# Masking one bank of scores on VectorE, computing it last, and moving the input sums in an attention and feed-forward kernel

## The chip, the cores and the metric

The kernel runs on one core of a Trainium2 chip. The metric is the device time of one execution in microseconds (us). Three runs of the kernel before took 1059.14, 1061.83 and 1064.9 us, so the median is 1061.83 us. TensorE (PE in the profile, with PEld for its weight loads) does the matrix products, ScalarE (ACT) the exponentials and copies out of PSUM, VectorE (DVE) reductions and subtractions, GpSimd (POOL) masks and other elementwise work, and SyncE (SP) issues nearly all transfers (DMAs).

## What is computed

One block with two parallel branches on a normalized input. Everything in it is float32; the attention is causal with a window of 256 keys.

```python
S, D, H, W, Df = 2048, 640, 32, 256, 1728
xn = layernorm(x)
q, k, v = split_heads(xn @ wqkv)                      # 32 heads of 20
scores = einsum("bhqd,bhkd->bhqk", q, k) * 20 ** -0.5
mask = (i - j >= 0) & (i - j < 256)
o = softmax(where(mask, scores, -1e9)) @ v
h = gelu(xn @ w_gate) * (xn @ w_up)
out = x + o @ wo + h @ w_down
```

## The kernel before

**Stages.** First the input is normalized and transposed, and split into a high and a low part (`xh`, `xl`), so that each float32 product is made of three fast ones. Then `attention()` runs from about 76 us to 583 us. Then the rest of the gate and up products follows (to about 818 us), and the output products to the end.

**Units and slots.** `attention()` works through 32 units: 8 groups of 4 heads by 4 chunks of 512 queries (`c = u % 4`). A unit takes 14 slots. In a slot the program writes out, in this order: what was put off to this slot (`tick`), pairs of score products for the row maximum (`pull_max`, in slots 0, 5 and 9), in slot 0 also the product with v of the unit before (`av_unit`), in the odd slots 1 to 11 two pieces of scores with their exponential (`exp_piece`), and a share of "filler" (`pull_fill`): the projections of q, k and v and the first gate and up products, 15 matrix products of 512 columns each, at `RATE / 14` of them per slot. PE, ACT, DVE and POOL run exactly in the written order here; SP's order is chosen by a scheduler. An engine that waits holds up everything behind it.

**Banks of scores.** A unit has 12 pieces, four heads by three banks (`pieces`). With b the chunk's first block of 128 keys, X holds keys b (384 queries) and b-2 (128), Y keys b+1 (384) and b+3 (128), and Z keys b-1 (256) and b+2 (256). Before, they are computed in the order X, Z, Y: X in slots 1 and 3, Z in 5 and 7, Y in 9 and 11. One slot after a bank's last piece `clear` sets what lies outside the window to zero, by selects on POOL over 128 keys x 4 heads x 128 queries (L558 on the diagonal, L561 at the far edge): three for X, two for Z, three for Y. A unit with c = 0 has two, one and three.

**The product with v.** `av_unit` in slot 0 of the next unit goes through half blocks of 64 keys, in the order of the banks (`steps_`). Its two accumulators (`os`) lie in the same two PSUM buffers that `exp_piece` uses.

**Row maxima.** `max_pair` makes scores in two PSUM banks (`ps_m`, of four), and DVE reduces each with the additive mask (L490) before the banks are free for the pair after next. In slot 0 two pairs stand ahead of `av_unit` and two behind it.

**Loads of q and k.** `load_stack(u + 3)` brings three copies of q and of k into SBUF, six transfers each. There are three q buffers and four k buffers. The k part is issued in slot 9 (KSLOT), the q part in slot 12. The k buffer that it fills is last read by this unit's pieces with keys of the chunk before (b-2 in X, b-1 in Z). The first pair that needs unit u + 3 is in slot 5 of unit u + 1.

**Sums of the input.** `x_sums` makes, on POOL, sums and differences of halves of the input that a later stage uses (80 operations of 128 x 256, tile `tx`) and stores them (`td`). There are eight such groups of ten operations, each group spread over 20 slots; group i starts at slot 24 + 50 i (XS0, XSN). The whole of `attention()` has 462 slots.

Of the kernel before, what the change touches and what calls it, by code (L numbers as in the profile page):

```python
# [9 lines left out]
F32 = mybir.dt.float32  # L10
# [3 lines left out]
OP = mybir.AluOpType  # L14
# [5 lines left out]
C = 512  # L20
# [7 lines left out]
NEG = -3.0e38  # L28
SR = 3 * DH
QROWS = 64 + SR  # L30
NS = 14
RATE = 35.3
V1_SLOT = 169
MXD = 7
KSLOT = 9
LAG = 3, 5, 4, 4, 4, 4, 3, 3, 4, 3, 2, 1, 1, 1
NFA = 4
HD = D // 2
# [1 line left out]
NQD = 9  # L40
OWN = 4, 5
WARM = 64
XS0, XSN = 24, 50
RAMP = 4.0
GAP = 16
VW = 1408
# [19 lines left out]
def block_kernel(ctx, tc, x, wqk, wv, wgu, wdo, wdl, out):  # L66
    nc = tc.nc
# [51 lines left out]
    qkp = pa.enter_context(tc.tile_pool(name="qkp", bufs=2))  # L119
    pr = ExitStack()  # L120
    vp = pr.enter_context(tc.tile_pool(name="vp", bufs=5, side="right"))
    st1 = pr.enter_context(tc.tile_pool(name="st1", bufs=1, side="right"))
    identb = st1.tile([128, 256], BF, name="identb")[:, 0:128]
    nc.gpsimd.tensor_copy(identb, ident)
    mask = st1.tile([128, 320], F32, name="mask")
    low = qkp.tile([128, C], F32, name="r", tag="r", bufs=1)[:, 0:320]
    for m, off in ((mask, 0), (low, 64)):
        nc.gpsimd.memset(m, 0.0)
        nc.gpsimd.affine_select(out=m, in_=m, pattern=[[1, 320]], compare_op=OP.is_ge,
                                fill=NEG, base=off - 1, channel_multiplier=-1)  # L130
        nc.gpsimd.affine_select(out=m, in_=m, pattern=[[-1, 320]], compare_op=OP.is_ge,
                                fill=NEG, base=256 - off, channel_multiplier=1)
    nc.gpsimd.tensor_copy(mask[64:128], low[64:128])
    pp = ExitStack()
# [63 lines left out]
    def at(slot, fn, *a):  # L198
        acts.setdefault(slot, []).append((fn, a))
# [17 lines left out]
    def defer(n, fn, *a):  # L217
        if now[0] is None:
            fn(*a)
        else:  # L220
            at(now[0] + n, fn, *a)
# [224 lines left out]
    def load_stack(u, which=(0, 1)):  # L446
        g, c = divmod(u, NC)
        for m in range(80 * g // 128, (80 * g + 79) // 128 + 1):
            assert all((m + 5 * i, c) in done for i in which), (u, m)

        for i in which:
            dst, src, top, again = ((qs[u % NQ], qd[c], 1, 2), (ks[u % NK], kd[c], 0, 0))[i]
            for j in (0, 2):
                for p, part, n in ((j * 32, top, 2), (j * 32 + 2 * DH, again, 1), (64 - j * 32, 0, 3)):
                    nc.sync.dma_start(dst[p:p + DH * n, j:j + 2].rearrange("p j t -> p (j t)"),
                                      src[g, part:part + n].rearrange("s (d j) t -> (s d) (j t)",
                                                                      j=4)[:, j * C:(j + 2) * C])
# [54 lines left out]
    def pieces(c):  # L512
        b = 4 * c
        X = [(b, 0, 0, 384)] + ([(b - 2, 384, 0, 128)] if c else [])
        Y = [(b + 1, 0, 128, 384), (b + 3, 384, 384, 128)]
        Z = ([(b - 1, 0, 0, 256)] if c else []) + [(b + 2, 256, 256, 256)]
        return X, Z, Y

    def diag_tail(kb, col, q0, n, c):
        r = []  # L520
        for i in range(n // 128):
            dist = 4 * c + q0 // 128 + i - kb
            if dist == 0:
                r.append((col + 128 * i, True))
            elif dist == 2:
                r.append((col + 128 * i, False))
        return r
# [23 lines left out]
    def clear(u, bi):  # L551
        c = u % NC
        pt = pts[u, bi]
        for p in pieces(c)[bi]:
            for col, diag in diag_tail(*p, c):
                a = pt[:, :, col:col + 128]
                if diag:
                    nc.gpsimd.affine_select(out=a, in_=a, pattern=[[0, 4], [1, 128]], compare_op=OP.is_ge,  # L558
                                            fill=0.0, base=0, channel_multiplier=-1)
                else:  # L560
                    nc.gpsimd.affine_select(out=a, in_=a, pattern=[[0, 4], [-1, 128]], compare_op=OP.is_ge,  # L561
                                            fill=0.0, base=-1, channel_multiplier=1)

    def av_unit(u):
        g, c = divmod(u, NC)
        v = vtiles[g]
        os = [psx.tile([128, C], F32, name="ps_o", tag="ex") for _ in range(2)]
        place = {kb - 4 * c: (pts[u, bi], col, q0) for bi, bank in enumerate(pieces(c)) for kb, col, q0, n in bank}

        def half(d, r):  # L570
            i = 2 * d + r
            return d, r, max(0, 64 * i), min(C, 64 * i + 320)

        steps_ = [((0, 0), (0, 1)), ((2, 0), (-1, 1)), ((-1, 0), (2, 1)), ((1, 0), (1, 1)),
                  ((3, 0), (-2, 1)), ((-2, 0), (3, 1))]
        todo = [half(*x) for pair in steps_ for x in pair if x[0] in place]
        begun_, left = set(), [sum(t[1] == r for t in todo) for r in range(2)]
        for d, r, qa, qb in todo:
            pt, col, q0 = place[d]
            kb = 4 * c + d  # L580
            assert (id(v), kb) in done, (u, kb)
            left[r] -= 1
            rows = slice(64 * r, 64 * r + 64)
            for j in range(4):
                w0_ = kb * 84 + 21 * j
                nc.tensor.matmul(os[r][32 * j:32 * j + 32, qa:qb], v[rows, w0_:w0_ + 32],  # L586
                                 pt[rows, j, col + qa - q0:col + qb - q0], start=r not in begun_,
                                 stop=not left[r], skip_group_check=True, tile_position=(64 * r, 32 * j))
            begun_.add(r)
        ob, oc = ap.tile([128, C], F32, name="ob", tag="ob", bufs=1), pts[u, 2][:, 0]  # L590
        lo = 0 if c else 64
        nc.scalar.activation(ob, os[0], AF.Copy)  # L592
        nc.scalar.activation(oc[:, lo:], os[1][:, lo:], AF.Copy)

        def join():
            nc.gpsimd.tensor_tensor(out=ob[:, lo:], in0=ob[:, lo:], in1=oc[:, lo:], op=OP.add)

        def store():
            for j in range(4):
                nc.sync.dma_start(od[c].rearrange("(d h) t -> h d t", h=H)[4 * g + j], ob[32 * j:32 * j + DH, :])  # L600
            nc.sync.dma_start(sd[c][4 * g:4 * g + 4, :], ob[DH::32, :])

        defer(3, join)
        defer(5, store)
# [161 lines left out]
    NU = NG * NC  # L766
# [4 lines left out]
    def pull_max(n, slot):  # L771
        for _ in range(n):
            x = next(stream, None)
            if x is None:
                return
            max_pair(*x)
            if x[1] == 7:
                at(slot + (MXD if slot >= 0 else 4), max_end, x[0])

    def tick():  # L780
        todo = [y for t in sorted(t for t in acts if t <= now[0]) for y in acts.pop(t)]
        return sorted(todo, key=lambda y: y[0] is max_end)
# [6 lines left out]
    def attention():  # L789
        now[0] = -1  # L790
        load_stack(0)
        load_stack(1)
        load_stack(2)
        for i, (p, k, half) in enumerate((p, k, half) for p in range(NC // 2) for k in range(2) for half in range(2)):
            for j, fn in enumerate(x_sums(p, k, half)):
                at(XS0 + XSN * i + 2 * j, fn)
        for i in range(12):
            now[0] = i - 13
            for fn, a in tick():
                fn(*a)  # L800
            if i % 2 == 0:
                pull_max(2, now[0])
            flush()
            pull_fill(2 * RAMP)
        pull_fill(GAP)
        for u in range(NU + 1):
            for i in range(NS):
                T = now[0] = NS * u + i
                for fn, a in tick():
                    fn(*a)  # L810
                if i in (0, 5, 9) or T == 3:
                    pull_max(2, T)
                if i == 0 and u:
                    av_unit(u - 1)
                    flush()
                    pull_max(2, T)
                if i % 2 and i < 12 and u < NU:
                    exp_piece(u, i - 1)
                    if i == 1 and u:
                        pull_fill(1)  # L820
                        debt[0] -= 1
                    exp_piece(u, i)
                flush()
                if u + 3 < NU and i in (KSLOT, 12):
                    load_stack(u + 3, (int(i == KSLOT),))
                pull_fill(RATE / NS)
        while acts:
            now[0] += 1
            for fn, a in tick():
                fn(*a)  # L830
            flush()
        now[0] = None
        run(fill)
        assert not acts
# [578 lines left out]
    for n, (p, k) in enumerate(steps):  # L1413
        i = n % (NQD + 1)
# [71 lines left out]
```

## Time and profile before

| | us |
|---|---|
| three runs | 1059.14, 1061.83, 1064.9 |
| profiled execution, its own time | 1063.24 |
| span in that profile | 1061.5 |
| PE busy | 1040.6 |
| DVE busy | 737.3 |
| ACT busy | 529.4 |
| POOL busy | 372.5 |

The span is the time from the first to the last instruction in the profile; the execution's own time is 1.7 us more. Busy time of PE is modelled (products are pipelined), so a busy PE isn't a PE at its peak. A row of the waits names who waited, for whom, and the total. In rows of the timeline the first two numbers are the start and the length in us; idle time of the engine just ahead and what ended it stand in brackets.

### The profile page before, as it was taken

How to read it: one execution, taken by the hardware profiler on the slowest of the kernel's cores; microseconds unless marked ns; L12 is line 12 of the kernel's file. 1: busy time of each engine (PE TensorE's matmuls, PEld its weight loads, DVE VectorE, ACT ScalarE, POOL GpSimd, SP SyncE). 2: the span in 40 equal slices, each digit the busy share in tenths (PEclk: the TensorE clock that was granted, in tenths of full speed). 3: DMA queues.
4: the chain of work that ended last, by engine and by line, in shares of the span. 5: the costliest groups of instructions: out<-in, count | busy, mean ns of one | idle time of the engine just before them, and what ended most of it. 6: DMA issues, size and time to landing. Idle time of an engine off the chain costs nothing.

```text
span 1061.5 us, 25594 instructions
## 1 busy us (share of the span) xinstructions
PE 1040.6 (98%) x9405; PEld 834.0 (79%) x9405; DVE 737.3 (69%) x2007; ACT 529.4 (50%) x1120; POOL 372.5 (35%) x534
## 2 busy tenths in 40 slices
PE   8999999999999999999999999999999999999998
PEld 8878656666678765666666888888888999999998
DVE  7845656665655666687674578877655879988887
ACT  4434667666566665666657532322334543433332
POOL 6021777877564658484846021110110000000000
PEclk9999999999999999999999999999999999999999
DMA  5643355564443335443422647576317874343433
GB/s 197 189 129 94 104 156 146 168 183 128 145 125 100 94 104 170 135 139 97 139 82 67 191 164 250 201 258 230 122 50 259 261 243 134 125 136 101 133 123 111
DMA packets 105191, 158.75 MB, mean 150 GB/s; under 512 B 15420, under 2 KB 60092, under 8 KB 105064
## 3 DMA queue, kind: packets, MB, share of 16 engines
q1 hardware_dynamic: 102680, 150.95, 44.4%
q10 hardware_dynamic: 2384, 6.16, 1.8%
q8 instruction: 74, 1.21, 0.5%
q14 instruction: 53, 0.43, 0.1%
HBM read 101.78 MB, written 54.92 MB: 148 GB/s over the span
## 4 chain that ended last, share of the span: by engine, by line
PE 77%; POOL 6%; DVE 6%; DMA 3%; ACT 3%; SPq 2%; issue 2%; ACTq 0%; DVEq 0%; POOLq 0%
PE ps_g L935 21%; PE ps L1202 17%; PE ps_d L105 17%; PE ps_v L105 6%; PE ps_e L545 6%; PE ps_o L586 4%; PE ps_m L480 4%; POOL pt L247 2%; POOL tx L724 1%; PE ps_g L105 1%; DVE junk L490 1%; POOL P L561 1%; ACT P L547 1%; POOL P L558 1%; POOL wql L627 1%
## 5 line engine op out<-in xcount | busy, mean ns | idle before, releaser
L490 DVE CUSTOM_DVE_ANT_0 junk<-ps_m,mask 128x320 bf16<-128x320 f32 (+2 forms) x512 | 243.1, 475 | 150.8 <-PE ps_m L480 94.4
L547 ACT ACTIVATE P<-ps_e 128x512 f32<-128x512 f32 (+2 forms) x384 | 198.8, 571 | 67.7 <-PE ps_e L545 66.1
L1202 PE MATMUL ps<-wb,at 128*128 128x320 f32 x999 | 156.9, 309 | 1.0 <-DVE at L1040 0.8
L1202 PEld LDWEIGHTS ps<-wb,at 128*128 128x128 f32 x999 | 148.9, 188 | 2.2 <-DVE at L1040 1.3
L545 PE MATMUL ps_e<-qs,ks 124*128 124x128 bf16 (+2 forms) x704 | 117.9, 278 | 1.2 <-ACT P L547 0.9
L558 POOL TENSOR_SCALAR_AFFINE_SELECT P<-P 128x512 f32<-128x512 f32 x128 | 83.4, 652 | 86.8 <-ACT P L547 82.7
L105 PE MATMUL ps_d<-xh,wqh 128*128 128x512 f32 x350 | 109.3, 420 | 0.0
L105 PE MATMUL ps_d<-xh,wql 128*128 128x512 f32 x350 | 108.7, 420 | 0.0
L105 PE MATMUL ps_d<-xl,wqh 128*128 128x512 f32 x350 | 108.4, 418 | 0.0
L1202 PE MATMUL ps<-wt,at 128*128 128x320 f32 x552 | 89.2, 310 | 0.8 <-DVE xr L1225 0.8
L545 PEld LDWEIGHTS <-ks 124*128 124x128 bf16 x704 | 49.7, 98 | 50.4 <-issue 37.3
L586 PE MATMUL ps_o<-P,v 64*32 64x320 f32 (+4 forms) x2816 | 77.6, 349 | 7.7 <-POOL P L561 7.4
L1202 PEld LDWEIGHTS ps<-wt,at 128*128 128x128 f32 x552 | 82.9, 188 | 1.4 <-DVE xr L1225 1.0
L1156 ACT ACTIVATE at<-ss 128x512 fp32r<-128x512 f32 x59 | 37.3, 632 | 86.6 <-DVE ss L1040 86.6
L561 POOL TENSOR_SCALAR_AFFINE_SELECT P<-P 128x512 f32<-128x512 f32 x112 | 72.3, 656 | 21.8 <-ACT P L547 21.8
L98 POOL TENSOR_TENSOR wql<-wr,wqh 128x640 fp32r<-128x640 f32 x11 | 17.6, 1606 | 174.1 <-PE ps_g L935 149.5
L586 PEld LDWEIGHTS ps_o<-P,v 64*32 64x32 f32 x2816 | 46.6, 106 | 36.8 <-POOL P L561 12.4
L105 PEld LDWEIGHTS ps_d<-xh,wql 128*128 128x128 f32 x350 | 64.4, 191 | 12.1 <-issue 1.4
L105 PEld LDWEIGHTS ps_d<-xl,wqh 128*128 128x128 f32 x350 | 63.8, 190 | 11.8 <-issue 1.5
L105 PEld LDWEIGHTS ps_d<-xh,wqh 128*128 128x128 f32 x350 | 63.7, 190 | 11.7 <-issue 1.9
L247 POOL TENSOR_TENSOR pt<-r,pt 128x512 bf16<-128x512 f32 x40 | 46.6, 1165 | 73.5 <-ACT pt L246 65.0
L592 ACT ACTIVATE ob<-ps_o 128x512 f32<-128x512 f32 x32 | 19.1, 598 | 92.7 <-PE ps_o L586 75.8
(195 smaller groups left out, 1923.3 us busy)
## 6 DMA issues: line engine op xcount, KB each, us to landing
hr<-hd SPq DMA_DIRECT2D x104, 128.0 KB
hd<-he SPq DMA_DIRECT2D x50, 256.0 KB
wr<-wgu SPq DMA_DIRECT2D x27, 320.0 KB
qs<-qd SPq DMA_DIRECT2D x64, 120.0 KB
ks<-kd SPq DMA_DIRECT2D x64, 120.0 KB
xi<-x SPq DMA_DIRECT2D x16, 320.0 KB
qs<-qd SPq DMA_DIRECT2D x64, 80.0 KB
ks<-kd SPq DMA_DIRECT2D x64, 80.0 KB
```

The costliest lines, as they stand in the source:

```text
L105: nc.tensor.matmul(ps, a(k), b(k), start=n == 0, stop=n == 3 * nk - 1)
L247: nc.gpsimd.tensor_tensor(out=pt[:, l, :], in0=r, in1=pt[:, 1, :], op=OP.subtract)
L480: nc.tensor.matmul(ps[64 * h:64 * h + 64, col:col + w], q[rows, j, q0:q0 + 64], ks_, start=True, stop=True, tile_position=(64 * r, 64 * h))
L490: nc.vector.tensor_tensor_reduce(out=junk[:, 0:n], in0=ps[:, 320 - n:320], in1=mask[:, 320 - n:320], scale=1.0, scalar=NEG, op0=OP.add, op ...
L545: nc.tensor.matmul(ps[:, col:col + n], k[0:QROWS, j, kc:kc + 128], q[0:QROWS, j, q0:q0 + n], start=True, stop=True)
L547: nc.scalar.activation(pt[:, j, lo:hi], ps[:, lo:hi], AF.Exp, scale=SCALE)
L558: nc.gpsimd.affine_select(out=a, in_=a, pattern=[[0, 4], [1, 128]], compare_op=OP.is_ge, fill=0.0, base=0, channel_multiplier=-1)
L561: nc.gpsimd.affine_select(out=a, in_=a, pattern=[[0, 4], [-1, 128]], compare_op=OP.is_ge, fill=0.0, base=-1, channel_multiplier=1)
L586: nc.tensor.matmul(os[r][32 * j:32 * j + 32, qa:qb], v[rows, w0_:w0_ + 32], pt[rows, j, col + qa - q0:col + qb - q0], start=r not in begun ...
L935: nc.tensor.matmul(ps, i, j, start=first and n == 0, stop=n == len(work) - 1, skip_group_check=True)
L1156: nc.scalar.activation(hi[:, 3:7], s, AF.Copy)
L1202: nc.tensor.matmul(ps[bank][:, 0:HD], *work[bank][j], start=bank not in begun, stop=final[p, bank] == n and j == len(work[bank]) - 1, skip ...
```

## The change

Five edits go together:

- The banks come in the order X, Y, Z, so the half-width bank Z is computed last (slots 9 and 11), and the product with v takes X, Y, Z.
- Z's masks leave POOL. `clear` does them on DVE: each 128 x 128 block that crosses an edge becomes two blocks of 64 keys x 4 heads x 64 queries, `min(P, mask + 3e38)`, with a mask of 0 or -3e38. The other corner blocks aren't read by the product with v. The mask tile grows from 320 to 324 columns for this.
- The sums of the input start at slot 170 and then every 33 slots, in place of 24 and every 50.
- Both q and k of unit u + 3 are loaded in slot 12, q first.
- The filler's rate falls from 35.3 to 34.8 products per unit.

```diff
-RATE = 35.3
+RATE = 34.8
-KSLOT = 9
+KSLOT = 12
-XS0, XSN = 24, 50
+XS0, XSN = 170, 33
@@ pieces
-        return X, Z, Y
+        return X, Y, Z
@@ clear
         pt = pts[u, bi]
+        if bi == 2:
+            for p in pieces(c)[bi]:
+                for col, diag in diag_tail(*p, c):
+                    for r in (0, 64):
+                        a = pt[r:r + 64, :, col + r:col + r + 64]
+                        m = mask[r:r + 64, 1:65] if diag else mask[r:r + 64, 257:321]
+                        m = m.rearrange("p (o t) -> p o t", o=1).to_broadcast([64, 4, 64])
+                        nc.vector.scalar_tensor_tensor(a, m, -NEG, a, op0=OP.add, op1=OP.min)
+            return
@@ av_unit
-        steps_ = [((0, 0), (0, 1)), ((2, 0), (-1, 1)), ((-1, 0), (2, 1)), ((1, 0), (1, 1)),
-                  ((3, 0), (-2, 1)), ((-2, 0), (3, 1))]
+        steps_ = [((0, 0), (0, 1)), ((1, 0), (1, 1)), ((3, 0), (-2, 1)), ((-2, 0), (3, 1)),
+                  ((2, 0), (-1, 1)), ((-1, 0), (2, 1))]
@@ attention
-                if u + 3 < NU and i in (KSLOT, 12):
-                    load_stack(u + 3, (int(i == KSLOT),))
+                if u + 3 < NU and i == KSLOT:
+                    load_stack(u + 3)
```

How the instructions move. On DVE, at the boundary between the second and the third unit, in the difference (a leading + is new; `r` is a step of saving a projection, the row below the new one is the first reduction of slot 0):

```order
 L490 ISA mx 128x1
 L261 TENSOR_TENSOR r<-ps_d,pt 128x512
+L561 SCALAR_TENSOR_TENSOR P<-mask,P 64x4x64 x4
 L490 ISA junk,mx<-ps_m,mask 128x320
 L490 ISA mx 128x1
```

The four masks stand ahead of slot 0's eight reductions in every full unit; whatever delays the masks delays these.

On PE, at the end of the last unit, before (`ps_e` are pieces of scores, `ps_o` the product with v, `ps_d` filler, `ps_g` the next stage):

```order
L545 LDWEIGHTS ks_188
L545 MATMUL ps_e<-qs_183,ks_188 128x384
L586 MATMUL ps_o<-P,v 32x320 x8
L586 MATMUL ps_o<-P,v 32x256 x8
L586 MATMUL ps_o<-P,v 32x192 x8
L586 MATMUL ps_o<-P,v 32x320 x8
L586 MATMUL ps_o<-P,v 32x128 x8
L586 MATMUL ps_o<-P,v 32x64 x8
L105 MATMUL ps_g<-xh_77,wqh 128x512 x5
```

and with the change:

```order
L545 LDWEIGHTS ks_188
L545 MATMUL ps_e<-qs_183,ks_188 128x256
L105 MATMUL ps_d<-xl_83,wqh 128x512 x5
L595 MATMUL ps_o<-P,v 32x320 x16
L595 MATMUL ps_o<-P,v 32x128 x8
L595 MATMUL ps_o<-P,v 32x64 x8
L595 MATMUL ps_o<-P,v 32x256 x8
L595 MATMUL ps_o<-P,v 32x192 x8
L105 MATMUL ps_g<-xh_77,wqh 128x512 x5
```

The filler's last five products, which stood in slot 5 of this unit, now stand behind its last piece. In the product with v the half blocks of Z (the 256 and 192 columns) are the last of 48 products in place of the second 16.

On SP, in an early unit's slot 12, before (`kd` and `qd` are the projections in DRAM, `pt` the tile they are stored from, `td` a sum of the input):

```order
L455 DMA ks_186<-kd_89 60x1024
L728 DMA td_103<-tx 128x256
L256 DMA kd_90<-pt 32x3x512
L256 DMA kd_90<-pt 80x3x512
L256 DMA kd_90<-pt 16x3x512
L455 DMA qs_184<-qd_85 40x1024
L455 DMA qs_184<-qd_85 20x1024
L455 DMA qs_184<-qd_85 60x1024
```

and with the change:

```order
L256 DMA kd_90<-pt 32x3x512
L256 DMA kd_90<-pt 80x3x512
L256 DMA kd_90<-pt 16x3x512
L455 DMA qs_184<-qd_85 20x1024
L455 DMA qs_184<-qd_85 60x1024
L455 DMA ks_186<-kd_89 40x1024
L455 DMA ks_186<-kd_89 20x1024
L455 DMA ks_186<-kd_89 60x1024
L455 DMA ks_186<-kd_89 40x1024
L455 DMA ks_186<-kd_89 20x1024
L455 DMA ks_186<-kd_89 60x1024
```

The six transfers of k follow the six of q, and the stores of `td` are gone from this early part.

More of the change, by code (lines that the diff above doesn't have):

```diff
@@ L124, in block_kernel @@
     nc.gpsimd.tensor_copy(identb, ident)
-    mask = st1.tile([128, 320], F32, name="mask")
-    low = qkp.tile([128, C], F32, name="r", tag="r", bufs=1)[:, 0:320]
+    mask = st1.tile([128, 324], F32, name="mask")
+    low = qkp.tile([128, C], F32, name="r", tag="r", bufs=1)[:, 0:324]
     for m, off in ((mask, 0), (low, 64)):
         nc.gpsimd.memset(m, 0.0)
-        nc.gpsimd.affine_select(out=m, in_=m, pattern=[[1, 320]], compare_op=OP.is_ge,
+        nc.gpsimd.affine_select(out=m, in_=m, pattern=[[1, 324]], compare_op=OP.is_ge,
                                 fill=NEG, base=off - 1, channel_multiplier=-1)
-        nc.gpsimd.affine_select(out=m, in_=m, pattern=[[-1, 320]], compare_op=OP.is_ge,
+        nc.gpsimd.affine_select(out=m, in_=m, pattern=[[-1, 324]], compare_op=OP.is_ge,
                                 fill=NEG, base=256 - off, channel_multiplier=1)
```

## The prediction

> **What bounds the kernel now.** I read the page's engine shares first, then busy time by stage, then the list of waits, then the timeline at several unit boundaries.
>
> ```profile
> span 1061.5 us, 25594 instructions
> PE 1040.6 (98%) x9405; PEld 834.0 (79%) x9405; DVE 737.3 (69%) x2007; ACT 529.4 (50%) x1120; POOL 372.5 (35%) x534
> ...
> POOL 6021777877564658484846021110110000000000
> ...
> 110.00:250.00 140.00, 135.34 (x1670) 87.49 (x1672) 87.30 (x324) 93.84 (x188) 109.01 (x158) 1.00 0.51 149
> 250.00:360.00 110.00, 108.36 (x1523) 81.10 (x1507) 65.54 (x259) 67.80 (x185) 65.16 (x104) 1.00 0.40 121
> 360.00:425.00 65.00, 63.36 (x801) 41.76 (x799) 40.40 (x152) 41.92 (x85) 43.49 (x64) 1.00 0.46 133
> 425.00:575.00 150.00, 149.63 (x1897) 99.89 (x1883) 100.24 (x341) 95.18 (x192) 88.53 (x132) 1.00 0.36 110
> 575.00:583.60 8.60, 6.93 (x120) 3.85 (x118) 5.52 (x8) 5.97 (x12) 8.01 (x10) 1.00 0.32 106
> ```
>
> In the window rows the busy times are PE, PEld, DVE, ACT, POOL; the granted clock is 1.00 throughout. PE bounds everything, so the change, which leaves PE's products as they are, can only gain where PE is idle. Inside attention that is 4.7 us from 110 to 250, 1.6 in each of the next two stretches, 0.4 in the long late one, and 1.7 in the last 8.6 us. POOL is 78% busy in the first of these stretches. The waits say whom PE waited for:
>
> ```profile
> POOL P L558 <- ACT P L547: 82.7, 44, 4.1
> ...
> PEld ps_o L586 <- POOL P L561: 12.4, 13, 1.7
> ...
> PE ps_o L586 <- POOL P L561: 7.4, 11, 1.4
> ...
> PEld ps_o L586 <- POOL P L558: 5.9, 15, 0.5
> ```
>
> (who, for whom: us in total, times, longest.) Eleven times the product with v waited for a mask of POOL. One of them in the timeline:
>
> ```profile
> 186.12 0.72 POOL L724 TENSOR_TENSOR tx<-xh,tx 128x256 f32<-128x256 f32 x1
> 186.61 1.53 PE L586 MATMUL ps_o<-P,v 64*32 64x320 f32 x48
> 186.92 0.73 POOL L724 TENSOR_TENSOR tx<-tx,xl 128x256 f32<-128x256 f32 x1
> 187.60 0.63 POOL L558 TENSOR_SCALAR_AFFINE_SELECT P<-P 128x512 f32<-128x512 f32 x1
> 188.19 0.63 POOL L561 TENSOR_SCALAR_AFFINE_SELECT P<-P 128x512 f32<-128x512 f32 x1
> ...
> 188.87 1.15 PE L586 MATMUL ps_o<-P,v 64*32 64x320 f32 x48 [0.74 <-POOL P L561]
> ```
>
> Two operations on the input sums stand ahead of the last bank's three selects, so the selects end too late. This product took from 186.61 to 190.02, 3.41 us; one that doesn't wait takes 2.45 (quoted below, at 493.83). So 0.74 us of idle time cost 0.96 us: 0.22 more than the idle time shows.
>
> **The change part by part.**
>
> *Masks off POOL, Z last, sums later: -9.9, of which I give 0.9 back.* The eleven waits cost 7.4 + 11 x 0.22 = 9.8 us, and 0.1 for the few where only the weight loads waited. The bounds are 7.4 (idle time alone) and 18.3 (all idle time of the weight loads for POOL). What now masks late on POOL is Y, in slot 8 and not 12, six slots (about 6.6 us at 15.4 us a unit) ahead of its use. POOL's load falls too:
>
> ```profile
> L561 POOL TENSOR_SCALAR_AFFINE_SELECT P<-P 128x512 f32<-128x512 f32 x112 | 72.3, 656 | 21.8 <-ACT P L547 21.8
> ...
> L724 POOL TENSOR_TENSOR tx<-tx,xl 128x256 f32<-128x256 f32 x48 | 35.1, 731 | 0.9
> ```
>
> 56 selects go (8 groups x (3 x 2 + 1)), 56 x 0.656 = 37 us in all; of the 80 sums at 0.731 us about 28 leave the stretch from 110 to 250, 20 us, with some 10 us of selects, so POOL's 109 us become about 79 of 140. The stretch from 360 to 425, where the last projections of q and k run, keeps one and a half groups of sums where it had one: there POOL stays as full as it was, and I leave one of the eleven waits standing: 0.9 back.
>
> *The filler lasts to the end: -1.2.* At 34.8 per unit the filler runs out in slot 11 of the last unit and not in slot 5, as the order shows. The tail before:
>
> ```profile
> 577.97 0.87 PE L545 MATMUL ps_e<-qs,ks 124*128 124x128 bf16 x4 [0.59 <-ACT P L547]
> 579.09 0.87 PE L545 MATMUL ps_e<-qs,ks 124*128 124x128 bf16 x4 [0.26 <-ACT P L547]
> 580.25 1.90 PE L586 MATMUL ps_o<-P,v 64*32 64x320 f32 x48 [0.29 <-ACT P L547]
> 582.45 1.20 PE L586 MATMUL ps_o<-P,v 64*32 64x320 f32 x48 [0.31 <-POOL P L561]
> ```
>
> The three waits for ACT, 1.14 us, are covered by filler that is done anyway; the fourth is among the eleven. The rate costs nothing elsewhere: 16 products leave the 31 full units and stand at their end, on the same engine. Bounds 0 and -1.5.
>
> *The masks on DVE: +3.2.* 112 instructions of 64 x 256. The trace has none; by elements per partition the nearest are these:
>
> ```profile
> L1040 DVE TENSOR_TENSOR ss<-hr 128x256 f32<-128x256 f32 x59 | 24.9, 422 | 1.3
> ...
> L661 DVE SCALAR_TENSOR_TENSOR he<-he,gs 128x512 f32<-128x512 f32 x16 | 13.1, 818 | 1.1
> ```
>
> I take 0.42 us; 0.82 is the upper end. That is 1.7 us in a full unit and 47 us in all, on an engine that has about a third of its time free. What counts is the place. They wait for ACT's last exponential, and slot 0's reductions wait behind them. A light boundary:
>
> ```profile
> 491.70 1.09 ACT L547 ACTIVATE P<-ps_e 128x512 f32<-128x512 f32 x2 [0.46 <-PE ps_e L545]
> 491.99 0.69 DVE L661 SCALAR_TENSOR_TENSOR he<-he,gs 128x512 f32<-128x512 f32 x1
> 493.81 0.49 DVE L490 CUSTOM_DVE_ANT_0 junk<-ps_m,mask 128x320 bf16<-128x320 f32 x1 [1.13 <-PE ps_m L480]
> 493.83 2.45 PE L586 MATMUL ps_o<-P,v 64*32 64x320 f32 x96
> 496.21 0.47 PE L480 MATMUL ps_m<-ks,qs 60*64 60x320 bf16 x8
> ```
>
> The exponential ends at 492.79, when DVE is free, so the masks end at 494.47. Z is needed after 65% of the columns of the product with v, at 493.83 + 0.65 x 2.45 = 495.42: 0.95 to spare. The reductions begin 0.66 later; a pair's two take 1.2 (0.64 from one start to the next at this place), so its banks are free at 495.7, ahead of their next use at 496.21. This boundary costs nothing, and DVE's idle 1.13 us is the cover. A heavy one, where DVE has two long steps of a gate product in front:
>
> ```profile
> 462.95 1.02 DVE L661 SCALAR_TENSOR_TENSOR he<-he,gs 128x512 f32<-128x512 f32 x1
> 463.37 1.08 POOL L558 TENSOR_SCALAR_AFFINE_SELECT P<-P 128x512 f32<-128x512 f32 x1
> 463.82 2.45 PE L586 MATMUL ps_o<-P,v 64*32 64x320 f32 x96
> 466.19 0.49 PE L480 MATMUL ps_m<-ks,qs 60*64 60x320 bf16 x8
> ```
>
> The masks run from 463.97 to 465.65, Z is needed at 465.41: 0.24 late. The first pair's banks come free at 466.85, wanted at 466.43 by then: 0.42 late. Together 0.65 us. Going through the boundaries in this way, DVE is over 1 us behind the exponential at seven of 31, three of them at chunks of half as many masks: 4 x 0.65 + 3 x 0.2 = 3.2 us. The bounds are 0 and the rival below.
>
> *k behind q on SP: +0.8.* Slot 12 now issues twelve transfers.
>
> ```profile
> 493.10 1.55 SPq L455 DMA_DIRECT2D qs<-qd  x4
> ...
> 500.75 0.37 PE L480 MATMUL ps_m<-ks,qs 60*64 60x64 bf16 x12
> ...
> 205.62 2.18 SPq L455 DMA_DIRECT2D qs<-qd  x6
> ...
> 210.42 0.47 PE L480 MATMUL ps_m<-ks,qs 60*64 60x256 bf16 x16
> ...
> 169.56 2.54 DMA ks<-kd
> ```
>
> Six issues take 2.2 us and the slowest landing of k on the chain 2.5. In the late unit q's last issue ends at 494.65, so k would be there at 499.4, 1.4 us ahead of the pair in slot 5 that reads it first. In the early one 207.80 becomes 212.5, and the pair stands at 210.42: 2.1 us late. There SP came to q only 3.9 us after the last exponential, held by stores of the sums and projections; the former leave. I charge 0.8 for all, bounds 0 and the rival below. Queued behind these issues are the stores of the attention output in slot 5, seven slots on, so these lose nothing.
>
> The sum is -9.9 + 0.9 - 1.2 + 3.2 + 0.8 = -6.2 us: a span of 1061.5 - 6.2 = 1055.3. The profiled execution's own time was 1063.24, 1.4 above the median of the runs; against the median I forecast 1061.83 - 6.2 = **1055.6 us**.
>
> **The rivals.**
>
> *The wait only changes its owner.* If DVE is behind at half of the 24 full boundaries, 12 x 0.65 = 7.8 replaces 3.2: -1.6, 1060.2 us. For it speaks that gate products keep DVE at 100 of 150 us late; against it that most boundaries show about 1 us of idle DVE.
>
> *Masks and POOL block each other: slower.* In the heavy boundary L661 took 1.02 us beside a select that took 1.08, against 0.69 and 0.63 when they ran alone. If every mask meets an operation of POOL, each is 0.35 longer, a unit's four end 1.4 later, and even the light boundary loses 0.45 at Z and 0.45 at the banks: 24 x 0.9 = 22 us in place of 3.2, so +12.6 and 1074 us. It decides from the point where a mask takes over 0.42 + 0.95 / 4 = 0.66 us. Against it: POOL is now off in slot 12 but for weight splits and sums. The Trainium skill, SBUF — State Buffer, "Who interferes with whom", has this as a rule: a VectorE instruction with two SBUF inputs contends with a GpSimd instruction that reads SBUF, and whoever starts first holds the port for its whole length. By that rule the masks (P and the mask tile, both in SBUF) are always open to it, and the trace agrees in the pair of rows at 462.95 and 463.37.
>
> *k late in each unit: slower.* If k lands 0.8 us too late after each of the 29 loads, 23 us replace 0.8: 1078 us. It decides once k needs over 1.4 us more than in my late unit. The early unit speaks for it; against it the late one, and that SP has less ahead of q once the stores of the sums are gone.
>
> **How the numbers follow.** What can be told from no change is about 0.5%, 5.3 us. I give the forecast 0.57, the wait that changes its owner 0.21, blocking 0.13, late k 0.09. So faster 0.57, same 0.21, slower 0.22. The forecast's own range is 1050.7 (all gains, no cost: -11.1) to 1058. With the lowest run, 2.7 below the median, the lower end is 1048. The upper end goes past the changed owner to the greater part of the blocking case: 1072.
>
> **What would show it.** Right: the wait of the product with v for POOL is gone or under 1 us; masks of about 0.42 us; PE idle in the stretch from 110 to 250 down from 4.7 to about 1; no wait of the `ps_e` products for ACT at the tail. Wrong: the product with v waiting over 4 us in total for DVE's P; the `ps_m` products waiting for DVE's reductions by 5 us or more; masks above 0.66; `ps_m` products waiting for the load of ks; POOL's waits returning in the stretch where sums and the last projections meet.

## Result and profile after: slower by 3.4%, lost behind the product with v

Four runs of the changed kernel took 1094.97 to 1101.01 us, median 1097.75; the kernel before, beside them, 1061.35. The ratio is 1.034 (95% interval 1.030 to 1.038), some 36 us slower where 6 us faster was forecast. Everything that was lost was lost in attention: from the first to the last copy of its output (L592 before, L601 after) 473.8 us became 509.5. What follows took 478 and 479 us, and what stands ahead of the first copy 109.9 and 106.5.

The page of the changed kernel, its first lines, to be held against those of before in the prediction:

```profile
span 1095.3 us, 25710 instructions
...
PE 1060.2 (97%) x9405; PEld 844.2 (77%) x9405; DVE 796.2 (73%) x2119; ACT 530.0 (48%) x1120; POOL 342.8 (31%) x478
```

PE has the same 9405 products. POOL lost 30 us of work and DVE gained 59. That is little of either engine's free time, so shares of busy time do not show the loss. The busy time by stretch does (PE, PEld, DVE, ACT, POOL, granted clock, DMA):

```profile
110.00:250.00 140.00, 134.26 (x1604) 88.12 (x1604) 100.59 (x338) 90.26 (x183) 80.71 (x113) 1.00 0.47 136
250.00:360.00 110.00, 106.69 (x1432) 78.06 (x1431) 75.03 (x272) 65.89 (x173) 56.39 (x90) 1.00 0.39 119
360.00:425.00 65.00, 60.84 (x754) 40.52 (x752) 45.28 (x150) 36.06 (x80) 38.30 (x54) 0.97 0.38 108
425.00:575.00 150.00, 142.05 (x1676) 92.05 (x1675) 110.17 (x361) 84.60 (x171) 86.09 (x123) 0.97 0.40 122
```

PE now idles 5.7, 3.3, 4.2 and 8.0 us in these stretches (4.7, 1.6, 1.6 and 0.4 before), most where it had hardly idled. POOL's 80.7 us in the first stretch is what the prediction had (79), so POOL was relieved as foreseen, and the total shows nothing of it. The waits of PE and of its weight loads in the kernel before (who, for whom: total us, times, longest) for the score pairs of the row maximum ("issue" is idle time for which the profile names no cause):

```profile
PEld L480 <- issue: 34.7, 106, 1.2
...
PE ps_m L480 <- DVE mx L490: 0.7, 2, 0.4
```

and in the changed kernel, with those of the product with v:

```profile
PEld L480 <- issue: 75.2, 195, 1.2
...
PE ps_m L480 <- DVE mx L490: 21.4, 64, 0.8
...
DVE P L561 <- ACT P L547: 13.4, 21, 1.3
...
PEld ps_o L595 <- DVE P L561: 1.0, 3, 0.4
...
PE ps_o L595 <- DVE P L561: 0.3, 1, 0.3
```

No product with v waits for POOL any more, and hardly any for the masks on DVE. The score pairs wait 64 times for a reduction. The idle time in the row of the weight loads grew by 40.5 us, that in PE's own by 20.7. PE's ends are modelled, so what follows goes by the starts of the weight loads.

The light boundary that the prediction went through (its second pull of score pairs began at 496.21) is this one now:

```profile
513.67 1.09 ACT L547 ACTIVATE P<-ps_e 128x512 f32<-128x512 f32 x2 [0.47 <-PE ps_e L545]
...
514.86 1.74 DVE L561 SCALAR_TENSOR_TENSOR P<-mask,P 64x256 f32<-64x256 f32 x4 [0.83 <-ACT P L547]
515.37 0.47 PE L480 MATMUL ps_m<-ks,qs 60*64 60x256 bf16 x16
515.78 2.55 PE L595 MATMUL ps_o<-P,v 64*32 64x320 f32 x96
516.63 0.69 DVE L663 TENSOR_TENSOR gs<-ps_d,gs 128x512 f32<-128x512 f32 x1
517.24 0.48 DVE L490 CUSTOM_DVE_ANT_0 junk<-ps_m,mask 128x320 bf16<-128x320 f32 x1
...
517.87 0.49 DVE L490 CUSTOM_DVE_ANT_0 junk<-ps_m,mask 128x320 bf16<-128x320 f32 x1
518.26 0.49 PE L480 MATMUL ps_m<-ks,qs 60*64 60x320 bf16 x4
...
518.52 0.49 DVE L490 CUSTOM_DVE_ANT_0 junk<-ps_m,mask 128x320 bf16<-128x320 f32 x1
...
519.07 0.29 PE L480 MATMUL ps_m<-ks,qs 60*64 60x320 bf16 x1 [0.32 <-DVE mx L490]
519.16 0.49 DVE L490 CUSTOM_DVE_ANT_0 junk<-ps_m,mask 128x320 bf16<-128x320 f32 x1
...
519.72 0.33 PE L480 MATMUL ps_m<-ks,qs 60*64 60x320 bf16 x3 [0.35 <-DVE mx L490]
519.97 0.50 PE L105 MATMUL ps_d<-xh,wqh 128*128 128x512 f32 x1
```

The masks took 1.74 us, as forecast (4 x 0.42), and the product with v did not wait for them. But a step of a gate product (L663) comes between the masks and the reductions, and the first reduction starts at 517.24, 1.9 us after its scores were begun. The second pull, two pairs in four banks, is written at 518.26; its first pair finds its banks just free, its second waits for the third and then for the fourth reduction. It lasts until 519.97: 1.71 us where 0.39 was enough before (496.21 to 496.60). From the first weight load of this pull to the next load of other work, summed over 30 boundaries, I get 15.2 us before and 53.1 after. These 37.9 us are more than the whole 35.7 that attention lost. From weight load to weight load, the product with v gives 6.9 back and the pieces of scores 1.4; the filler's products take 6.3 more (249.4 to 255.7 us), most of it while the clock was halved (last section).

### The profile page after: what moved, and what is told of

Read it like the earlier page. It is cut to its first block, busy times and chain, and to the rows that moved or that the text cites. A ratio compares the mean times of both kernels' runs of the same rounds, so it can differ in the third digit from the quotient of the medians.

```text
span 1095.3 us, 25710 instructions
## 1 busy us (share of the span) xinstructions
PE 1060.2 (97%) x9405; PEld 844.2 (77%) x9405; DVE 796.2 (73%) x2119; ACT 530.0 (48%) x1120; POOL 342.8 (31%) x478
## 4 chain that ended last, share of the span: by engine, by line
PE 73%; DVE 15%; ACT 4%; issue 4%; DMA 2%; POOL 1%; ACTq 0%; SPq 0%; DVEq 0%; POOLq 0%
PE ps_g L944 19%; PE ps_d L105 17%; PE ps L1211 15%; PE ps_e L545 7%; PE ps_v L105 6%; DVE junk L490 5%; DVE P L561 4%; PE ps_m L480 3%; PE ps_o L595 3%; ACT P L547 2%; PE ps_g L105 1%; DVE at L1049 1%; DVE wb L1049 1%; DVE ss L1049 1%; DVE r L261 1%
## 5 line engine op out<-in xcount | busy, mean ns | idle before, releaser
L105 PE MATMUL ps_d<-xl,wqh 128*128 128x512 f32 x350 | 110.9, 426 | 0.0
L480 PE MATMUL ps_m<-ks,qs 60*64 60x320 bf16 (+3 forms) x1472 | 78.5, 260 | 23.3 <-DVE mx L490 21.4
L480 PEld LDWEIGHTS <-qs 60*64 60x64 bf16 x1472 | 34.6, 105 | 79.2 <-issue 75.2
L567 POOL TENSOR_SCALAR_AFFINE_SELECT P<-P 128x512 f32<-128x512 f32 x96 | 61.9, 644 | 105.3 <-ACT P L547 105.3
L561 DVE SCALAR_TENSOR_TENSOR P<-mask,P 64x256 f32<-64x256 f32 x112 | 66.1, 590 | 16.1 <-ACT P L547 13.4
L105 PEld LDWEIGHTS ps_d<-xh,wqh 128*128 128x128 f32 x350 | 63.7, 191 | 10.9 <-issue 0.3
```

Source lines behind the costliest of these rows:

```text
L105: nc.tensor.matmul(ps, a(k), b(k), start=n == 0, stop=n == 3 * nk - 1)
L480: nc.tensor.matmul(ps[64 * h:64 * h + 64, col:col + w], q[rows, j, q0:q0 + 64], ks_, start=True, stop=True, tile_position=(64 * r, 64 * h))
L561: nc.vector.scalar_tensor_tensor(a, m, -NEG, a, op0=OP.add, op1=OP.min)
```

## The experiments

Each time stands beside runs of the kernel before on the same chip (1061.6 to 1062.1 us). The ratio is to those.

**All masks on POOL again, the other edits kept.**

```diff
-        if bi == 2:
-            for p in pieces(c)[bi]:
...
-                        nc.vector.scalar_tensor_tensor(a, m, -NEG, a, op0=OP.add, op1=OP.min)
-            return
```

> The changed kernel with the masks of bank Z back on POOL (two selects in place of four VectorE masks); order of banks, sums, loads and rate as changed. Theory A (the four masks delay slot 0's reductions on VectorE, so the second pull of score products waits for its PSUM banks): the loss of 36 us goes, and most of the gain forecast for the rest comes, 1052 to 1060 us, with PE ps_m waits for DVE under 4 us (21.4 in the changed kernel). Theory B (k loaded behind q, or the moved sums, are what costs): stays at 1090 or above.

1057.56 us, ratio 0.9964 (0.9951 to 0.9978). The second pull takes 16.9 us. So the masks on DVE cost 40 us (1097.75 less 1057.56), all of the loss; the other four edits together gain 4.

**Z's masks left out altogether** (its weights outside the window stay in the sum).

```diff
         if bi == 2:
-            for p in pieces(c)[bi]:
...
-                        nc.vector.scalar_tensor_tensor(a, m, -NEG, a, op0=OP.add, op1=OP.min)
             return
```

> The changed kernel with the masks of bank Z left out on any engine, so its output is not the reference's: the floor of everything but the masks. Theory A: 1048 to 1056 us, a little below the kernel with these masks on POOL. Theory B: 1090 or above.

1057.54 us, 0.9961 (0.9942 to 0.998), a little above theory A's range: the same as with the masks on POOL. On POOL, with the sums late, they cost nothing that can be measured. This is also all that any place for them could gain.

**The sums of the input early again, masks on DVE.**

```diff
-XS0, XSN = 170, 33
+XS0, XSN = 24, 50
```

> The changed kernel with the input's sums back at slot 24 and every 50. Theory A: VectorE's delay is at every boundary with or without the sums, so 1094 to 1104 us, the late part a little better and the early a little worse. Rival C (the sums moved to the late part run into the masks on the port between VectorE and POOL and lengthen them to 590 ns): 1075 to 1085 us, masks nearer 450 ns.

1102.0 us, 1.0375 (1.0353 to 1.0396). The late sums do not make the loss; without them it is a little larger. Nor do they alone lengthen the masks, as rival C had it: with the sums early a mask takes 596 ns in the mean, with the sums late 590.

**The order X, Y, Z and k in slot 12 alone** (the kernel before with these two edits, masks on POOL, sums and rate as they were).

```diff
-KSLOT = 9
+KSLOT = 12
-        return X, Z, Y
+        return X, Y, Z
```

(with the same order in `steps_` of `av_unit`)

> The kernel before with only the order of banks X, Y, Z and both loads in slot 12: all masks on POOL, sums and rate as before. Theory A: near the kernel before, 1056 to 1064 us, since POOL has two selects and not three at the end. Theory B (late k costs): 1075 us or above, with ps_m products waiting for the load of ks.

1069.91 us, 1.0072 (1.0047 to 1.0096), between the ranges of the two theories. The waits of the product with v for POOL stay, and grow:

```profile
PEld ps_o L586 <- POOL P L558: 11.9, 14, 1.9
...
PE ps_o L586 <- POOL P L558: 9.4, 12, 1.8
```

Z last has two selects in front of the product and not three, yet it waits 9.4 us where 7.4 were waited before: the sums on POOL ahead of them make them late. With the same order, the sums late and the rate lower (the first experiment) the wait is 2.2 us.

**The second pull moved from slot 0 to slot 2**, masks on DVE.

```diff
                     flush()
+                if i == 2 and u:
                     pull_max(2, T)
```

> The changed kernel, with the second pull of score products (two pairs) written in slot 2 and not behind the product with v in slot 0; masks still on VectorE. Theory A1 (the loss is PE standing at that second pull, because its second pair's banks are freed by the third and fourth reduction, which the masks delay): the pull now comes two slots later, the wait goes, 1056 to 1066 us, ps_m waits under 5 us (21.4). Rival A2 (VectorE is too slow over the whole unit, so that the wait turns up wherever the pull stands): 1085 us or above.

1077.43 us, 1.0154 (1.0139 to 1.017), between the ranges of A1 and A2. Half of the loss is gone; 20 us against all masks on POOL are left. Whether these were still the masks, the ninth run below tells.

**The same DVE instructions on spare data**: they read the mask tile alone, write a spare tile and wait for no exponential; Z stays unmasked.

```diff
-                        a = pt[r:r + 64, :, col + r:col + r + 64]
+                        junk = ap.tile([128, 320], BF, name="junk", tag="junk", bufs=1)
+                        a = mask[r:r + 64, 0:256].rearrange("p (o t) -> p o t", o=4)
...
-                        nc.vector.scalar_tensor_tensor(a, m, -NEG, a, op0=OP.add, op1=OP.min)
+                        nc.vector.scalar_tensor_tensor(junk[r:r + 64, 0:256].rearrange("p (o t) -> p o t", o=4),
+                                                       m, -NEG, a, op0=OP.add, op1=OP.min)
```

> The changed kernel with the four masks kept on VectorE at the same place and in the same size, but working on data that nobody waits for (mask tile in, a scrap tile out), so P is not masked in bank Z and the output is not the reference's. If it is the time that they take ahead of slot 0's reductions: 1085 to 1098 us. If it is that they wait for the last exponential and hold the reductions up until then: 1060 to 1072 us.

1089.57 us, 1.0263 (1.0244 to 1.0283). Against all masks on POOL 32 of the 40 us are still there. Most of what costs is the time on DVE ahead of the reductions. The other 8 go with waiting for the exponential; the split is rough, since the instructions took 70.7 us in all here and 66.1 in the changed kernel.

**Half of the masks on DVE** (the diagonal; the far edge again by a select on POOL, 64 of 112 instructions stay).

```diff
                 for col, diag in diag_tail(*p, c):
+                    if not diag:
+                        nc.gpsimd.affine_select(out=pt[:, :, col:col + 128], in_=pt[:, :, col:col + 128],
+                                                pattern=[[0, 4], [-1, 128]], compare_op=OP.is_ge,
+                                                fill=0.0, base=-1, channel_multiplier=1)
+                        continue
                     for r in (0, 64):
```

> The changed kernel with half of bank Z's masks on VectorE (the diagonal block, two instructions) and the far edge on POOL (one select). If the cost follows the time of the masks evenly: about 1077 us, the middle of 1057.6 (none on VectorE) and 1097.8 (all). If VectorE's idle time at the boundary covers the first ones: 1058 to 1066 us.

1074.0 us, 1.0118 (1.0103 to 1.0133): 57% of the masks cost 16.4 of the 40 us (41%). So the first masks are not free, and DVE's idle time covers a small part at most. The second pull takes 34.7 us here, 16.9 with the masks on POOL and 53.1 in the changed kernel. The score pairs' wait for reductions, 21.4 us in the changed kernel and 1.4 with the masks on POOL, is 10.8 here.

**Late sums and the lower rate alone**, on the kernel before.

```diff
-RATE = 35.3
+RATE = 34.8
-XS0, XSN = 24, 50
+XS0, XSN = 170, 33
```

> The kernel before with only the input's sums moved (slot 170, every 33) and the rate 34.8; banks in the order X, Z, Y, all masks on POOL, k loaded in slot 9. If the 12 us between the order alone (1069.9) and the change without VectorE masks (1057.6) belong to these two edits whatever the order: 1049 to 1055 us. If they only pay with Z last: 1058 to 1062 us.

1057.02 us, 0.9961 (0.9947 to 0.9975), between the two ranges, a lower median than either kernel's: 4.6 us under before by the medians, 4.1 by the ratio. It and the changed kernel with all masks on POOL are, with the one without Z's masks, the fastest that were run, and can't be told apart. The product with v waits for POOL 3.0 us in place of 7.4.

**The second pull in slot 2 with all masks on POOL**, the control to the fifth.

> The changed kernel with all masks on POOL and the second pull of score pairs in slot 2. With the masks on POOL and the pull in slot 0 the ratio was 0.9964; with the masks on DVE and the pull in slot 2 it was 1.0154. If the 20 us that the moved pull left are due to the masks' time on DVE over the whole unit, the pull's place costs nothing by itself: 1054 to 1060 us, weight loads of the score pairs about 49 to 52 us in all. If they are due to the new place of the pull (two pulls on DVE close together), they stay: 1070 to 1078 us with weight loads near 66 us.

1077.34 us, 1.0147 (1.0132 to 1.0161), the same as with the masks on DVE (1.0154). So the 20 us belong to the pull's new place, and once the pull is there, the masks on DVE cost nothing that shows. From each weight load to the next, in the order of the loads, the score pairs of the row maxima take 63.7 us and not 51.0 as with the pull in slot 0, and the small products of the maxima (L507) 4.7 and not 0.5: 17 of the 20 us. The trace shows where:

```profile
480.98 0.23 PE L507 MATMUL ps_n<-identb,nm 128*128 128x128 bf16 x1
...
481.14 0.76 PE L480 MATMUL ps_m<-ks,qs 60*64 60x320 bf16 x4
...
481.92 0.25 ACT L509 ACTIVATE mr<-ps_n 32x128 bf16<-32x128 f32 x1
...
482.22 0.29 PE L480 MATMUL ps_m<-ks,qs 60*64 60x320 bf16 x1 [0.32 <-DVE mx L490]
...
482.86 0.33 PE L480 MATMUL ps_m<-ks,qs 60*64 60x320 bf16 x3 [0.35 <-DVE mx L490]
...
483.12 0.39 PE L545 MATMUL ps_e<-qs,ks 124*128 124x256 bf16 x2
```

The program puts L507 seven slots behind the pull that ends a unit's maxima. With that pull in slot 2 it comes in slot 9 and not in slot 7, directly ahead of slot 9's pull, and its result takes one of the same four banks. The pull behind it lasts 1.98 us here; the 30 such pulls take 27.9 us in all, where with the pull in slot 0 the same loads take about 0.40 us each. So the edit moved two things, and PE waits in slot 9 in place of slot 0, with or without the masks.

**k loaded in slot 12 alone**, on the kernel before.

```diff
-KSLOT = 9
+KSLOT = 12
-                if u + 3 < NU and i in (KSLOT, 12):
-                    load_stack(u + 3, (int(i == KSLOT),))
+                if u + 3 < NU and i == KSLOT:
+                    load_stack(u + 3)
```

> The kernel before with one edit: the k part is loaded in slot 12 behind q. If k late is harmless, as the missing wait for it in the changed kernel suggests, the time is that of before within 0.3% (1058 to 1065 us), and the 7.8 us that the order alone with late k cost belong to the order X, Y, Z (the last bank's masks behind the sums on POOL). If late k is their cause, 1067 to 1071 us, with pairs in slot 5 waiting for the load.

1062.19 us, 1.0001 (0.999 to 1.0012). Late k costs nothing. So the 7.8 us of the fourth run belong to the order of the banks.

**The rate alone**, on the kernel before.

```diff
-RATE = 35.3
+RATE = 34.8
```

> The kernel before with the filler's rate at 34.8 alone. The prediction's term for it is 1.2 us: 1060 to 1061.5 us, and no wait of the last unit's pieces for the exponential. If instead the rate is the larger part of the 4.6 us that rate and late sums gained together, 1057 to 1058.5 us.

1061.3 us, 0.9998 (0.9979 to 1.0016): no gain that can be told.

**The late sums alone**, on the kernel before.

```diff
-XS0, XSN = 24, 50
+XS0, XSN = 170, 33
```

> The kernel before with the sums of the input alone at slot 170 and every 33. By the prediction's terms the sums free POOL early: the product with v waits for POOL's masks 3 to 4 us instead of 7.4 of idle time, and the time falls by 3 to 5 us, 1057 to 1059 us. If the rate made the gain, 1060 to 1063 us.

1058.75 us, 0.9974 (0.9961 to 0.9987): 2.8 us of the 4.1 that rate and sums gain together. The product with v waits 3.5 us for POOL.

## Why the prediction was wrong

The step that failed is the light boundary, in the part on the masks on DVE: "its banks are free at 495.7, ahead of their next use at 496.21. This boundary costs nothing, and DVE's idle 1.13 us is the cover". It followed the first pair alone, two banks. The second pull in slot 0 is two pairs, four banks, and PE writes all four within 0.39 us; its second pair needs the third and the fourth reduction of the pull before. By the prediction's own numbers the fourth ends at 494.47 + 4 x 0.64 = 497.0, some 0.6 us after it is wanted, with masks of 0.42 us and nothing in between. So by these numbers a full boundary isn't light: a second pull follows 22 of them, and 22 x 0.6 = 13 us. The trace of the changed kernel bears the size out. At the six of the 22 where the four masks took 1.68 us together, as forecast, the second pull lasted 1.14 us in the mean (0.46 to 1.71), about 0.7 over the 0.40 of an undisturbed one. At the other sixteen, with longer masks, it lasted 2.10. Steps of DVE between the masks and the reductions add to it, as at 516.63. 3.2 us became 40. That the masks cost at this place alone, the pair of runs with the second pull in slot 2 says: there they took nearly as long (557 ns in the mean) and cost 0.0007 of the time (1.0154 less 1.0147).

- **Masks off POOL, Z last, sums later: forecast -9.9 with 0.9 back.** The mechanism was right, the size came out only in the place looked at. From weight load to weight load, the product with v takes 80.9 us before, 74.0 after the change and 72.7 with Z's masks left out. But the order X, Y, Z without late sums is 7.8 us slower. The version without Z's masks holds this term, the rate and late k, forecast together at -9.4; it measured -4.1 us (0.9961), and with the masks on POOL the gain is the same. Of the 8.2 us that the product gained there, the score pairs take 4.9 back (48.0 to 52.9 us), 3.0 of them at the second pull (15.2 to 18.2); why was not tried.
- **The filler lasts to the end: forecast -1.2.** The waits for the exponential at the tail are gone in the changed kernel and with the rate alone, as foreseen, but alone the rate gave -0.2 us with an interval of about 2 on either side. It can't be told from nothing, nor from 1.2.
- **k behind q: forecast +0.8.** Late k alone: 1.0001, and in the changed kernel no score product waits for k. The rival "k late in each unit" falls.
- **Masks of 0.42 us, decided against at 0.66.** The row of all 112 (duration in ns: least, median, most):

```profile
L561 DVE SCALAR_TENSOR_TENSOR P<-mask,P x112: 404/423/1414, 103.9 to 614.5; 64x256 f32<-64x256 f32 x112
```

and as a group (busy us, mean ns of one, idle before):

```profile
L561 DVE SCALAR_TENSOR_TENSOR P<-mask,P 64x256 f32<-64x256 f32 x112 | 66.1, 590 | 16.1 <-ACT P L547 13.4 <-POOL tx L733 0.8
```

The median is the forecast; the mean of 590 lies below the 660 named for "masks and POOL block each other". Of the 112, 55 ran while no operation of POOL did and took 404 to 425 ns. The 44 that took over 500 ns all met one that had begun ahead of them, and each ended 0.28 us (0.275 to 0.287) after that operation's end. Ten that began ahead of POOL's operation took 416 to 424 ns. The rule of the Trainium skill, SBUF — State Buffer, "Who interferes with whom", which the prediction weighed (one side holds the port, the other waits), holds in these rows. The prediction had 0.35 us as the price of one meeting, read from L661 at 462.95 beside the select at 463.37. In that trace a sum on POOL (L724, 462.68 to 463.42) had begun ahead of L661, and the select began behind it; so a meeting costs about what is left of the POOL operation, and the longest mask was 1.0 us over the median. At its worst, in the changed kernel:

```profile
410.19 1.17 POOL L247 TENSOR_TENSOR pt<-r,pt 128x512 bf16<-128x512 f32 x1
...
410.67 3.32 DVE L561 SCALAR_TENSOR_TENSOR P<-mask,P 64x256 f32<-64x256 f32 x4 [0.53 <-ACT P L547]
...
411.31 0.92 POOL L733 TENSOR_TENSOR tx<-tx,xl 128x256 f32<-128x256 f32 x1
...
412.31 0.79 POOL L733 TENSOR_TENSOR tx<-xh,tx 128x256 f32<-128x256 f32 x1
```

Four masks took 3.32 us in place of 1.7. Blocking adds 112 x (590 - 423) ns = 19 us to DVE's work, and it stands ahead of the reductions. It makes the loss larger than the four banks alone would. No run kept the masks and cleared POOL. As an estimate from the trace: 16 x (2.10 - 1.14) at the full boundaries, and 4 x (1.90 - 1.27) at four of the eight with two masks where these were longer, make 18 of the 37.9 us. These boundaries also differ in DVE's other steps, so the share is not shown.
- **What would show it.** Of the signs named for a wrong forecast one came: score pairs waiting for reductions, 21.4 us where 5 was the mark. Of those for a right one, PE's idle time from 110 to 250 didn't fall to 1 but rose to 5.7. The sign named first, the product with v waiting over 4 us for the masks, stayed at 0.3. The cover was lost behind the place the prediction was watching.

## What to carry to other kernels

An engine that runs in written order gives no cover for work put ahead of a step that frees buffers. Count all the buffers that the next user fills in one go, and take the time at which the last of them comes free. Work moved off a busy helper is worth only the wait it ends: here 7 us at the product with v, at the price of 38 at the next pull. And an experiment that moves a wait needs its control: only the same move without the masks showed that the 20 us left were the move's own, because it had also moved L507 ahead of another pull.

## What the runs showed of the hardware

The granted clock of TensorE halved for 3.4 us at a time inside attention: four times in the profile of the changed kernel, at 418.3, 452.4, 486.6 and 537.8 us. Windows around these (the third number from the right is the mean clock):

```profile
410.00:425.00 15.00, 12.93 (x168) 7.93 (x166) 10.09 (x30) 6.90 (x14) 11.09 (x17) 0.89 0.54 151
440.00:455.00 15.00, 13.71 (x170) 8.38 (x169) 11.77 (x36) 8.07 (x17) 9.88 (x12) 0.91 0.51 150
485.00:500.00 15.00, 14.34 (x114) 9.02 (x118) 10.41 (x35) 8.16 (x18) 10.28 (x16) 0.89 0.25 77
530.00:545.00 15.00, 13.49 (x173) 8.78 (x172) 10.47 (x32) 6.62 (x13) 8.99 (x14) 0.89 0.42 133
```

The profile of the kernel before had none in attention. In the 3.4 us ahead of each, PE idled 1.0 to 2.0 us in all, and no single wait exceeded 0.9 us. For a wider look I laid a grid of 3.41 us through the clock's changes in all fourteen profiles, from 100 to 1050 us. Of eleven stretches in which PE idled over 1.4 us in all, eight were followed by a halved one; of 23 with 1.0 to 1.4 us, eight; of those with less only two, and these were halved already. The three over 1.4 us that were not followed by one (one in the run of the order alone, two in that of the rate alone) each had a single wait of 1.55 to 1.76 us. So here the halved clock went with idle time summed over a stretch, many short waits included, but the sum alone does not decide it. Four such stretches at half speed can cost up to 4 x 1.7 = 7 us of PE's time. The weight loads in them stand 4.7 us further apart in all than the median of their kind elsewhere in attention: as an estimate, that is their part of the 36 us.
